# The last product of the attention units beside the chunks: 32-bit operands on half the rows, in place of three terms of split halves

## The chip, the cores and the metric

The kernel runs on one core of a Trainium2 chip. The metric is the device time of one execution in microseconds (us), from the host's side of the launch; lower is better. In the profile PE is the matrix engine (TensorE), PEld its weight loads, DVE is VectorE, ACT is ScalarE, POOL is GpSimd, SP is SyncE, whose queue issues most DMAs.

## The reference, cut to what matters

```python
def sm_attn(qq, kk, vv):
    s = scale * np.matmul(qq, kk.transpose(0, 1, 3, 2))
    s = s - np.max(s, axis=-1, keepdims=True)
    a = np.exp(s)
    a = a / (np.sum(a, axis=-1, keepdims=True) + 1e-09)
    return np.matmul(a, vv)
p_packed = sm_attn(p, k, v)                  # 32 packed rows per head
out = sm_attn(q, p_packed, p_packed)         # batch 8, heads 8, seq 576, head_dim 64
...
k = np.maximum(xk @ w_k, 0.0)                # MoE-like mixer on the attention's output
v = k * k @ w_v
r = 1.0 / (1.0 + np.exp(-(xr @ w_r)))
x = r * v
...
u = x + (x.transpose(0, 2, 1) @ U @ V).transpose(0, 2, 1)
out = u + np.maximum(u @ w_ch1, 0.0) @ w_ch2
```

The change concerns only the last product of the attention, `a @ p_packed`, and only in half of the attention units. All results are float32.

## The kernel before, in words

**Units.** A unit is a pair of batches times a pair of heads (two batches, two heads, 576 positions); there are 16. The first 8, the lead, run ahead of everything else, overlapped by `LAG`. They are called plain (`NPLAIN = 8`, L515). The other 8, units 8 to 15, run beside the chunks: at chunk 5 and at chunk 8 (L1392 to L1396) four units each are put into the program, and their instructions are laid between the matrix products of the chunks.

**Chunks.** The attention's output goes to DRAM (`x_d`) and comes back in 12 chunks of 384 positions. Each chunk has products into the accumulators `psr` (`r_block`, 128x512), `psk` (`k_block`, 128x384), `psv` (`v_block`, 128x512) and `psu` (`xu_block`, 128x512). After the chunks comes the second mixer (`psc`), which fills more than half of the time.

**Operand types.** The chunks' products take operands split in halves: a value is rounded to the type `F32R` (high half), the rest is a second `F32R` (low half), and `PASS` (L517) lists the three terms that are summed, high x high, high x low, low x high. One such term is one matmul instruction in the profile. A product with plain `F32` operands is one instruction in the program and two (each with its own weight load) in the profile.

**The end of a unit.** `pp` holds the packed rows of both batches and both heads, block-diagonal for the heads, batch 0 on partitions 0 to 63, batch 1 on 64 to 127. `th` holds the attention's shares, transposed, in the same partitions. In a plain unit (L841 to L846) each batch has one `F32` product that contracts over its own 64 partitions, so it uses 64 of the array's 128 rows, and the two batches use different rows. In a unit beside the chunks (L847 to L853) the product contracts over all 128 partitions with a weight matrix `wide` (`ppz`) in which the other batch's 64 rows are zero, so that it has the shape of a chunk's product, in three terms:

```python
for n, (lh, rh) in enumerate(((0, th), (0, tl), (1, th))):
    plan.mm(pss[b2][:, 0:w], ppz[:, lh, b2, :], rh[:, c0:c1], start=(n == 0), stop=(n == 2))
```

The 576 positions go in two pieces, 320 and then 256 (`halves`, L777), because a PSUM bank holds 512 columns; so a unit has 4 outputs (2 pieces x 2 batches) and 12 terms. Each output is copied from its bank to `xo` by ACT or DVE (L854), and `xo` is stored to `x_d` by one DMA (L856). What the three terms need beside the products: the halves of `pp` (L757 to L760), the halves of `th` (L828 to L832), and the zeros of `wide`, written once (L1024).

**What sets the order.** Nothing is issued as it is written. Every operation is recorded in a `Plan`, and `emit` (L341) replays the record as a list scheduler: it has a cost for each operation, takes on each engine the ready operation with the lowest class and place, and gives out PSUM banks as they come free. The attention units beside the chunks have two of the eight banks (`ps_a`). All matrix products are issued at L197 (transposes at L209), all ACT copies at L288, DVE copies at L291, DVE additions and subtractions at L254, DMAs at L319. The resulting order of each engine is fixed in the program; engines wait for each other by semaphores. The planner's cost of a matmul (L195 to L205) depends on the operands' type and on the number of rows and columns of the array that it uses, so the order of the whole program follows from these numbers.

Of the kernel before, what the change touches and what calls it, by code (L numbers as in the profile page):

```python
# [9 lines left out]
F32 = mybir.dt.float32  # L10
F32R = mybir.dt.float32r
I32 = mybir.dt.int32
U32 = mybir.dt.uint32
AF = mybir.ActivationFunctionType
# [463 lines left out]
def packed_attention_moe_mixer_kernel(  # L478
# [18 lines left out]
    B, H, S, D = q.shape  # L497
    NP = p.shape[2]
    P = 128
# [20 lines left out]
    plan = Plan(nc)  # L520
    add, sub, mul = ALU.add, ALU.subtract, ALU.mult

    def open_pool(es, name, bufs, side):
        return es.enter_context(tc.tile_pool(name=name, bufs=bufs, side=side, reuse_waits="tile"))
# [32 lines left out]
    def ps_att():  # L557
        return plan.bank(att_banks[0], "psat", att_banks[0] is ps_a)
# [17 lines left out]
    class Bufs:  # L576
        def __init__(self, es, name, side, nbig, first=False):
            self.big_p = Pool(obj=open_pool(es, name + "big", nbig, side), bufs=nbig)
            one = open_pool(es, name + "one", 1, side)
            self.one = Pool(obj=one, bufs=1)  # L580
            self.a1 = plan.fixed(one.tile([P, 640], F32, name="a1"))
            self.pbd = plan.fixed(one.tile([P, 2, D], F32, name="pbd"))
            self.st = plan.fixed(one.tile([P, 16], F32, name="st"), (0, 1))
            self.wide = None if first else plan.fixed(one.tile([P, 2, 2, P], F32R, name="wide"), (0, 1))
            self.first = first
            self.pools = [self.big_p, self.one]
            for f in (self.a1, self.pbd, self.st) + (() if first else (self.wide,)):
                f.alloc = plan.add((), lambda: None)
                self.one.tiles.append(f)
            self.kin, self.qin, self.vin, self.after = {}, {}, {}, ()  # L590
            plan.zero(self.a1[:, 512:640])
            plan.ts(self.st.at(1)[:, 7:8], self.a1[:, 512:513], 1e-9, None, add)
            self.kept = None

        def keep(self, plain):
            if self.kept is None or self.kept[0] != plain:
                pT = plan.tile(self.one, [P, 2, 64], F32, "pT")
                self.kept = (plain, pT, self.wide)
            return self.kept[1:]

        def tile_in(self, tag):
            return plan.tile(self.big_p, [P, 1152], F32, "big", parts=(0, 1, 2, 3), name=tag)
# [44 lines left out]
    def attention_steps(A, u, u_next):  # L647
# [5 lines left out]
        plain = u < NPLAIN  # L653
        kh = A.big(F32, "kh")
        qt, at = A.big(F32, "qt"), A.big(F32, "at", (0, 1))
        pT, ppz = A.keep(plain)

        def claim():
            A.kin[u_next], A.qin[u_next], A.vin[u_next] = [A.tile_in(n) for n in ("kin", "qin", "vin")]
# [27 lines left out]
        for b2 in range(2):  # L687
            for h in range(2):
                o = slice(b2 * 64 + h * 32, b2 * 64 + (h + 1) * 32)
                for r in range(2):  # L690
# [3 lines left out]
                            start=True, stop=True, skip_group_check=True)  # L694
# [15 lines left out]
        for b2 in range(2):  # L710
            r = slice(b2 * 64, (b2 + 1) * 64)
# [5 lines left out]
        for c in range(3):  # L717
# [5 lines left out]
            n = 3 if c < 2 or not plain else 2  # L723
            w = 8 if plain else NI
# [21 lines left out]
        for t in range(5):  # L746
            for g in range(4):
# [4 lines left out]
                        start=(t == 0), stop=(t == 4), skip_group_check=True)  # L752
        pp = plan.tile(A.one, [P, P], F32, "pp")
        plan.stt(pp.rearrange("p (h d) -> p h d", h=2), ps[:, 0:D].unsqueeze(1).to_broadcast([P, 2, D]),
                 s0[:, 9:10], hmask, mul, mul)
        if not plain:
            for b2 in range(2):  # L757
                r = slice(b2 * 64, (b2 + 1) * 64)
                plan.copy(ppz.at(b2)[r, 0, b2, :], pp[r])
                plan.tt(ppz.at(b2)[r, 1, b2, :], pp[r], ppz.at(b2)[r, 0, b2, :], sub)  # L760
        if early:
            A.load_v(u_next, A.after)
        yield
# [14 lines left out]
        if plain:  # L778
            yield
            psa = ps_att()  # L780
            for ip in range(4):
                for b2 in range(2):
                    plan.mm(psa[:, ip * P + b2 * 64:ip * P + (b2 + 1) * 64],
                            qt[:, b2 * 512 + ip * P:b2 * 512 + (ip + 1) * P],
                            ppt[:, b2 * 64:(b2 + 1) * 64], start=True, stop=True)
            yield
            psb = ps_att()
            plan.mm(psb[:, 0:P], qt[:, 1024:1152], ppt, start=True, stop=True)
            if A.first:
                a2 = A.big(F32, "a2", (0, 1))[:, 0:20 * NP].rearrange("p (g k) -> p g k", k=NP)  # L790
            else:
                a2 = plan.tile(A.one, [P, 20, NP], F32, "a2", parts=(0, 1))
            s2 = plan.tile(A.one, [P, 4, 20], F32, "s2", parts=(0, 1))
            for g, src, g0, g1 in ((0, psa, 0, 16), (1, psb[:, 0:P], 16, 20)):
                sv = src.rearrange("p (g k) -> p g k", k=NP)
                plan.reduce(s2.at(g)[:, 0, g0:g1], sv, ALU.max)
                plan.tt(a2.on(g)[:, g0:g1, :], sv,
                        s2.at(g)[:, 0, g0:g1].unsqueeze(2).to_broadcast([P, g1 - g0, NP]), sub)
            shares(a2, s2, 20)

            a2f = a2.rearrange("p g k -> p (g k)")
            th, tl = A.big(F32, "th"), None
            yield
            ps = ps_att()
            for ip in range(4):
                plan.transpose(ps[:, ip * P:(ip + 1) * P], a2f[:, ip * P:(ip + 1) * P], ident)
            plan.copy(th[:, 0:512], ps)
            yield
            ps = ps_att()
            plan.transpose(ps[:, 0:P], a2f[:, 512:640], ident)  # L810
            for b2 in range(2):
                r = slice(b2 * 64, (b2 + 1) * 64)
                plan.copy(th[r, 512:576], ps[r, r])
        else:
            n = S // NP
            a2 = plan.tile(A.one, [P, 20, NP], F32, "a2", parts=(0, 1))[:, 0:n, :]
            s2 = plan.tile(A.one, [P, 4, 20], F32, "s2", parts=(0, 1))
            for g, (c0, c1) in enumerate(halves):
                yield
                ps = ps_att()  # L820
                for b2 in range(2):
                    plan.mm(ps[b2 * 64:(b2 + 1) * 64, 0:c1 - c0], ppt[:, b2 * 64:(b2 + 1) * 64],
                            qt[:, b2 * S + c0:b2 * S + c1], start=True, stop=True, skip_group_check=True)
                plan.turn(a2.on(g)[:, c0 // NP:c1 // NP, :].rearrange("p g k -> p (g k)"), ps[:, 0:c1 - c0])
            plan.reduce(s2[:, 0, 0:n], a2, ALU.max)
            plan.tt(a2, a2, s2[:, 0, 0:n].unsqueeze(2).to_broadcast([P, n, NP]), sub)
            shares(a2, s2, n)
            tw = A.big(F32R, "th", (0, 1))  # L828
            th, tl = tw.at(0)[:, 0:S], tw.at(1)[:, S:2 * S]
            plan.turn(qt[:, 0:S], a2.rearrange("p g k -> p (g k)"))  # L830
            plan.act(th, qt[:, 0:S], AF.Copy)
            plan.tt(tl, qt[:, 0:S], th, sub)  # L832
            yield
        xo = A.big(F32, "xo", (0, 1)).rearrange("p (i b c) -> p i b c", i=NI, b=2)
        if u_next is not None and A.first:
            claim()
# [2 lines left out]
            A.load_v(u_next)  # L839
        for c0, c1 in halves:  # L840
            w = c1 - c0  # L841
            if plain:
                yield
                pss = [ps_att() for _ in range(2)]
                for b2 in range(2):
                    r = slice(b2 * 64, (b2 + 1) * 64)  # L846
                    plan.mm(pss[b2][:, 0:w], pp[r, :], th[r, c0:c1], start=True, stop=True)  # L847
            for b2 in range(2):
                if not plain:
                    yield  # L850
                    pss = {b2: ps_att()}
                    for n, (lh, rh) in enumerate(((0, th), (0, tl), (1, th))):
                        plan.mm(pss[b2][:, 0:w], ppz[:, lh, b2, :], rh[:, c0:c1], start=(n == 0), stop=(n == 2))  # L853
                plan.copy(xo.on(b2)[:, c0 // 64:c1 // 64, b2, :],  # L854
                          pss[b2][:, 0:w].rearrange("p (i c) -> p i c", c=64))
        x_last[0] = plan.dma(x_d[bp].at(j)[j * P:(j + 1) * P, :], xo.rearrange("p i b c -> p (i b c)"))  # L856
# [3 lines left out]
    def attention(A, u, u_next):  # L860
        for _ in attention_steps(A, u, u_next):
            pass
# [71 lines left out]
    A0 = Bufs(es_att, "A", "right", 8)  # L934
# [84 lines left out]
    for b2 in range(2):  # L1019
        r = slice(b2 * 64, (b2 + 1) * 64)  # L1020
        z = A0.a1[r, 513 - b2:577 - b2:2]
        plan.copy(ust[r].rearrange("p i (a c) -> p (i a) c", c=32),
                  z.unsqueeze(1).to_broadcast([64, NI * 4, 32]), ("dve",))
        plan.copy(A0.wide[r, :, 1 - b2, :].rearrange("p l (a c) -> p l a c", c=32),  # L1024
                  z.unsqueeze(1).unsqueeze(1).to_broadcast([64, 2, 4, 32]), ("dve",))
    usv = ust.rearrange("p i (a b r) -> p i a b r", a=2, b=2)
    uv = U.rearrange("(p i) r -> p (i r)", i=NI)
    for i0, i1 in ((0, NI),):
# [268 lines left out]
    bank_abc, first, acc = {}, set(), {}  # L1297
# [92 lines left out]
    for n in range(2, len(chunks)):  # L1390
        b, c = chunks[n]
# [63 lines left out]
    for q in range(NQ):  # L1455
# [11 lines left out]
        for f in range(NF):  # L1467
# [4 lines left out]
            a = product(q, f, 0, "a", True)  # L1472
# [5 lines left out]
            c = product(q, f, 2, "c", True)  # L1478
# [67 lines left out]
```

## Time and profile before

| | |
|---|---|
| median of 3 runs (lowest, highest) | 1498.82 us (1495.47 to 1500.59) |
| the profiled execution's own time | 1496.43 us |
| its span, first to last instruction | 1494.6 us |
| PE busy, PEld busy | 1462.0 us (98%), 1284.5 us (86%) |
| DVE, ACT, POOL busy | 926.5 us (62%), 685.7 us (46%), 269.1 us (18%) |
| share of PE in the chain that ended last | 92% |
| lead, chunks with attention, chunks alone, second mixer | about 0 to 137, 137 to 520, 520 to 700, 700 to 1495 us |

How to read it: a busy PE means that some matmul was in flight; a matmul's record is longer than its place in the stream, since it overlaps the next one. What a matmul costs the stream is read from the starts: the start of the next one less its own.

### The profile page before, as it was taken

The numbers are of one execution on the slowest core, as the hardware profiler recorded it, in microseconds if no ns is written. First come the engines' busy times: TensorE is split into PE (matmuls) and PEld (weight loads), VectorE is DVE, ScalarE is ACT, GpSimd is POOL, SyncE is SP. The second block draws the span as 40 slices with busy tenths as digits, with TensorE's granted clock in tenths as the row PEclk, the third lists the DMA queues.
The fourth block names the chain that finished last, engine by engine and source line by source line (L and its number), as shares of the span: only waits on it lengthen the run. The fifth ranks groups of instructions, "written<-read, shape, count | busy, mean of one in ns | idle before, by whom it ended". The sixth has DMA issues, their size and how long they took to land.

```text
span 1494.6 us, 25540 instructions
## 1 busy us (share of the span) xinstructions
PE 1462.0 (98%) x9336; PEld 1284.5 (86%) x9336; DVE 926.5 (62%) x2104; ACT 685.7 (46%) x1561; POOL 269.1 (18%) x522
## 2 busy tenths in 40 slices
PE   6899999999999999999999999999999999999998
PEld 5667888888888888888899999999999999999997
DVE  6777967888888888786544454544445454443533
ACT  5677666676666666775332322223232232322221
POOL 0000000000000000001333333333333233333331
PEclk8899999999999999999999999999999999999999
DMA  8963344654654448576969686686768667676763
GB/s 234 251 197 106 107 133 125 196 166 141 199 177 144 140 141 268 177 246 187 293 169 240 168 232 158 184 226 174 227 156 234 160 180 222 165 216 156 204 173 102
DMA packets 202188, 275.65 MB, mean 184 GB/s; under 512 B 68944, under 2 KB 95888, under 8 KB 202064
## 3 DMA queue, kind: packets, MB, share of 16 engines
q0 software_dynamic: 72576, 132.15, 33.5%
q1 hardware_dynamic: 129488, 141.87, 30.8%
q8 instruction: 75, 1.23, 0.3%
q14 instruction: 49, 0.40, 0.1%
HBM read 221.45 MB, written 52.50 MB: 183 GB/s over the span
## 4 chain that ended last, share of the span: by engine, by line
PE 92%; DMA 3%; DVE 2%; ACT 1%; SPq 1%; issue 1%; DVEq 0%; ACTq 0%
PE psc L197 50%; PE psk L197 13%; PE psv L197 13%; PE psr L197 7%; PE psat L197 4%; PE psat L209 3%; PE psh L197 1%; PE pst L209 1%; PE psu L197 1%; SPq L319 1%; DMA x_d<-xo 1%; DMA kin<-in_k_dram 1%; DMA s<-w_d 1%; DMA qin<-in_q_dram 1%; DMA prs<-x_d 0%
## 5 line engine op out<-in xcount | busy, mean ns | idle before, releaser
L197 PE MATMUL psc<-w,hid 128*128 128x512 f32 x1728 | 419.8, 391 | 0.7 <-ACT xu L288 0.7
L197 PEld LDWEIGHTS psc<-ob,wb 128*128 128x128 f32 x3024 | 388.3, 191 | 14.5
L197 PE MATMUL psc<-ob,wb 128*128 128x256 f32 x3024 | 398.8, 283 | 0.0
L319 POOL DMA_DIRECT2D wb<-ws_d x504 | 266.2, 528 | 580.2 <-PE psc L197 463.2
L197 PEld LDWEIGHTS psc<-w,hid 128*128 128x128 f32 x1728 | 315.3, 189 | 60.2 <-ACT xu L288 1.0
L254 DVE TENSOR_TENSOR tmp<-tmp,psc 128x256 f32<-128x256 f32 x288 | 120.3, 418 | 152.8 <-PE psc L197 150.6
L197 PE MATMUL psk<-xk,wk 128*128 128x384 f32 x1056 | 208.5, 340 | 1.2 <-ACT sq L233 0.8
L197 PE MATMUL psv<-wv,kk 128*128 128x512 f32 x783 | 202.0, 395 | 0.0
L233 ACT ACTIVATE hid<-tmp 128x256 fp32r<-128x256 f32 x216 | 85.7, 416 | 238.9 <-DVE tmp L254 238.9
L197 PEld LDWEIGHTS psk<-xk,wk 128*128 128x128 f32 x1056 | 184.6, 188 | 10.6 <-issue 1.5
L197 PEld LDWEIGHTS psv<-wv,kk 128*128 128x128 f32 x783 | 144.3, 188 | 28.3 <-issue 0.8
L273 DVE SCALAR_TENSOR_TENSOR hid<-psc,hid 128x256 fp32r<-128x256 f32 x72 | 30.5, 424 | 187.1 <-ACT hid L233 187.1
L197 PE MATMUL psr<-wr,xr 128*128 128x512 f32 x414 | 111.1, 401 | 0.1
L233 ACT ACTIVATE hid<-psc 128x256 fp32r<-128x256 f32 x72 | 27.4, 381 | 180.3 <-PE psc L197 180.3
L273 DVE SCALAR_TENSOR_TENSOR hid<-tmp,hid 128x256 fp32r<-128x256 f32 x216 | 87.2, 422 | 22.7 <-ACT hid L233 13.9
L311 POOL MEMSET x<- 128x8 f32 x4 | 0.4, 112 | 530.0 <-DVE m L270 529.7
L197 PEld LDWEIGHTS psr<-wr,xr 128*128 128x128 f32 x414 | 75.2, 188 | 18.3 <-issue 3.2
L233 ACT ACTIVATE sq<-psk 128x384 f32<-128x384 f32 x96 | 46.5, 489 | 69.1 <-PE psk L197 66.6
L288 ACT ACTIVATE tmp<-psc 128x256 f32<-128x256 f32 x144 | 54.3, 377 | 51.7 <-PE psc L197 51.7
L254 DVE TENSOR_TENSOR kk<-sq,kk 128x384 fp32r<-128x384 f32 x87 | 47.9, 553 | 33.7 <-ACT kk L288 33.4
L270 DVE SCALAR_TENSOR_TENSOR m<-x,mu_t,m 128x384 f32<-128x384 f32 x88 | 51.7, 611 | 1.1 <-ACT m L233 1.1
L233 ACT ACTIVATE m<-x,om_t 128x384 f32<-128x384 f32 x88 | 50.8, 607 | 2.7 <-DVE xr L254 1.8
(174 smaller groups left out, 1657.2 us busy)
## 6 DMA issues: line engine op xcount, KB each, us to landing
wb<-ws_d POOLq DMA_DIRECT2D x504, 256.0 KB, 3.5
st<-in_moe_w_ch_dram SPq DMA_DIRECT2D x32, 512.0 KB, 5.2
ws_d<-wb SPq DMA_DIRECT2D x56, 256.0 KB, 2.9
qin<-in_q_dram SPq DMA_DIRECT2D x32, 288.0 KB, 5.4
x_d<-xo SPq DMA_DIRECT2D x16, 576.0 KB, 3.5
x_d<-x SPq DMA_DIRECT2D x36, 256.0 KB, 2.1
u<-x_d SPq DMA_DIRECT2D x36, 256.0 KB, 5.3
out_dram<-u SPq DMA_DIRECT2D x36, 256.0 KB, 2.3
```

The lines of the kernel that those rows point to most:

```text
L197: self.nc.tensor.matmul(o, l, r, start=start, stop=stop, **k)
L209: self.nc.tensor.transpose(out.get(), in_.get(), ident.get())
L233: self.nc.scalar.activation(o, in_.get(), func, **k)
L254: return self.elem(engs, lambda e, o, x, y: e.tensor_tensor(out=o, in0=x, in1=y, op=op), out, [a, b], self.TT, cls)
L270: ("dve",), lambda e, o, x, y, z: e.scalar_tensor_tensor(out=o, in0=x, scalar=z, in1=y, op0=op0, op1=op1), out, [a, b, s], {"dve": (1.042, ...
L273: ("dve",), lambda e, o, x, y: e.scalar_tensor_tensor(out=o, in0=x, scalar=s, in1=y, op0=op0, op1=op1), out, [a, b], self.TT, cls)
L288: self.nc.scalar.activation(o, i, AF.Copy)
L311: (self.nc.gpsimd if eng == "pool" else self.nc.vector).memset(o, 0.0)
L319: (self.nc.sync if eng == "sp" else self.nc.gpsimd).dma_start(out=o, in_=i)
```

## The change

The units beside the chunks end like the plain ones. `wide`, its zeros, its halves and the halves of `th` go; the transposed shares are written to `th` directly as `F32`; each of the 4 outputs of a unit is one `F32` product over 64 rows, and the two batches of a piece are requested together, with two banks.

```diff
-            self.wide = None if first else plan.fixed(one.tile([P, 2, 2, P], F32R, name="wide"), (0, 1))
...
-        if not plain:
-            for b2 in range(2):
-                r = slice(b2 * 64, (b2 + 1) * 64)
-                plan.copy(ppz.at(b2)[r, 0, b2, :], pp[r])
-                plan.tt(ppz.at(b2)[r, 1, b2, :], pp[r], ppz.at(b2)[r, 0, b2, :], sub)
...
-            tw = A.big(F32R, "th", (0, 1))
-            th, tl = tw.at(0)[:, 0:S], tw.at(1)[:, S:2 * S]
-            plan.turn(qt[:, 0:S], a2.rearrange("p g k -> p (g k)"))
-            plan.act(th, qt[:, 0:S], AF.Copy)
-            plan.tt(tl, qt[:, 0:S], th, sub)
-            yield
+            th = A.big(F32, "th")
+            plan.turn(th[:, 0:S], a2.rearrange("p g k -> p (g k)"))
...
-            if plain:
-                yield
-                pss = [ps_att() for _ in range(2)]
-                for b2 in range(2):
-                    r = slice(b2 * 64, (b2 + 1) * 64)
-                    plan.mm(pss[b2][:, 0:w], pp[r, :], th[r, c0:c1], start=True, stop=True)
+            yield
+            pss = [ps_att() for _ in range(2)]
             for b2 in range(2):
-                if not plain:
-                    yield
-                    pss = {b2: ps_att()}
-                    for n, (lh, rh) in enumerate(((0, th), (0, tl), (1, th))):
-                        plan.mm(pss[b2][:, 0:w], ppz[:, lh, b2, :], rh[:, c0:c1], start=(n == 0), stop=(n == 2))
+                r = slice(b2 * 64, (b2 + 1) * 64)
+                plan.mm(pss[b2][:, 0:w], pp[r, :], th[r, c0:c1], start=True, stop=True)
+            for b2 in range(2):
                 plan.copy(xo.on(b2)[:, c0 // 64:c1 // 64, b2, :],
                           pss[b2][:, 0:w].rearrange("p (i c) -> p i c", c=64))
...
-        plan.copy(A0.wide[r, :, 1 - b2, :].rearrange("p l (a c) -> p l a c", c=32),
-                  z.unsqueeze(1).unsqueeze(1).to_broadcast([64, 2, 4, 32]), ("dve",))
```

Since the planner sees other costs, the order changes in more places than the diff shows. On PE, at the end of the first unit beside the chunks, the order before is this (`th` with `wide` are the three-term products of the unit, `psv` and `psr` the chunk's; x6 means six instructions in a row):

```order
L197 MATMUL psv<-wv_1865,kk 128x512 x3
L197 MATMUL psat<-th,wide 128x320 x2
L197 MATMUL psv<-wv_1865,kk 128x512
L197 MATMUL psr<-wr_184,xr 128x512 x2
L197 MATMUL psv<-wv_1865,kk 128x512 x2
L197 MATMUL psat<-th,wide 128x320 x4
L197 MATMUL psv<-wv_1865,kk 128x512 x3
L197 MATMUL psr<-wr_184,xr 128x512
L197 MATMUL psr<-wr_185,xr 128x512 x2
L197 MATMUL psat<-th,wide 128x256 x6
L197 MATMUL psr<-wr_185,xr 128x512
```

And this is PE at the end of the same unit with the change (`th` with `pp` are the 32-bit products; each is two instructions in a profile):

```order
L197 MATMUL psv<-wv_1873,kk 128x512 x7
L197 MATMUL psat<-th,pp 128x320 x2
L197 MATMUL psv<-wv_1873,kk 128x512 x2
L197 MATMUL psr<-wr_181,xr 128x512 x2
L197 MATMUL psat<-th,pp 128x256
L197 MATMUL psr<-wr_181,xr 128x512
L197 MATMUL psat<-th,pp 128x256
L197 MATMUL psr<-wr_182,xr 128x512 x3
```

The three groups of like-shaped terms became one pair for the piece of 320 and, for the piece of 256, two single products with a chunk's matmul between them. Five of the eight units have this form. In the other three (here the third) the piece of 256 is a pair too:

```order
L197 MATMUL psk<-xk,wk_0_185 128x384 x2
L197 MATMUL psat<-th,pp 128x320 x2
L197 MATMUL psk<-xk,wk_0_185 128x384
L197 MATMUL psk<-xk,wk_0_186 128x384 x3
L197 MATMUL psk<-xk,wk_0_187 128x384 x2
L197 MATMUL psat<-th,pp 128x256 x2
L197 MATMUL psk<-xk,wk_0_187 128x384
```

So all eight pieces of 320 stand as pairs, three pieces of 256 as pairs and five as two singles: 21 groups in the chunks' stream, each with chunk products on either side. In the lead the orders of PE, DVE and ACT differ from about a third of the lead on, with the same operations less the two zero copies of `wide`; the orders of SP's queue in the lead and of POOL's are the same.

## Rows read from the trace of the kernel before

**Rows 1.** Busy time by stretch: length, PE, PEld, DVE, ACT, POOL, clock, DMA share, GB/s.
```profile
60.00:137.00 77.00, 70.07 (x650) 50.25 (x649) 60.92 (x150) 57.56 (x155) 0.00 (x0) 0.99 0.59 173
137.00:520.00 383.00, 380.29 (x2442) 326.93 (x2443) 315.21 (x696) 256.20 (x538) 0.22 (x2) 1.00 0.50 154
```
**Rows 2.** Chain that ended last: start us, length us, what, matmuls in the piece.
```profile
205.73 5.44 PE psr L197 x24
...
357.00 2.10 PE psk L197 x12
```
**Rows 3.** Timeline of PE, 269.5 to 272 us: start, length, form, count, idle before.
```profile
269.33 0.63 PE L197 MATMUL psu<-xs,ust 128*128 128x512 f32 x2
270.47 0.50 PE L197 MATMUL psu<-xs,ust 128*128 128x512 f32 x1 [0.52 <-DVE xs L291]
271.41 0.50 PE L197 MATMUL psu<-xs,ust 128*128 128x512 f32 x1 [0.44 <-DVE xs L254]
271.74 0.51 PE L197 MATMUL psk<-xk,wk 128*128 128x384 f32 x2
```
**Rows 4.** Timeline of PE at the end of the first unit beside the chunks.
```profile
252.42 0.84 PE L197 MATMUL psv<-wv,kk 128*128 128x512 f32 x3
253.10 0.45 PE L197 MATMUL psat<-th,wide 128*128 128x320 f32 x2
253.39 0.39 PE L197 MATMUL psv<-wv,kk 128*128 128x512 f32 x1
...
254.55 0.75 PE L197 MATMUL psat<-th,wide 128*128 128x320 f32 x4
255.14 0.86 PE L197 MATMUL psv<-wv,kk 128*128 128x512 f32 x3
...
256.53 0.87 PE L197 MATMUL psat<-th,wide 128*128 128x256 f32 x6
257.24 0.88 PE L197 MATMUL psr<-wr,xr 128*128 128x512 f32 x3
```
**Rows 5.** Instructions on tile `wide`: count, duration ns min/median/max, first and last start.
```profile
L197 PE MATMUL psat<-th,wide x96: 277/294/313, 253.1 to 507.0; 128*128 128x320 f32 x48, 128*128 128x256 f32 x48
L254 DVE TENSOR_TENSOR wide<-pp,wide x16: 276/286/290, 238.7 to 489.5; 64x128 fp32r<-64x128 f32 x16
```
**Rows 6.** Instructions on tile `th`, same columns: its halves.
```profile
L233 ACT ACTIVATE th<-qt x8: 668/676/687, 250.2 to 502.8; 128x576 fp32r<-128x576 f32 x8
L254 DVE TENSOR_TENSOR th<-qt,th x8: 751/756/760, 252.1 to 503.5; 128x576 fp32r<-128x576 f32 x8
```
**Rows 7.** Timeline of PE where the last plain unit ends between chunk products.
```profile
134.73 1.03 PE L197 MATMUL psk<-xk,wk 128*128 128x384 f32 x5
135.69 1.24 PE L197 MATMUL psat<-th,pp 64*128 64x320 f32 x8
136.87 0.45 PE L197 MATMUL psk<-xk,wk 128*128 128x384 f32 x1
137.15 0.34 PE L197 MATMUL psk<-xr,wk 128*128 128x384 f32 x1
```
**Rows 8.** Timeline of PE, another plain unit: the pair of 320.
```profile
108.64 0.81 PE L197 MATMUL psat<-th,pp 64*128 64x320 f32 x4
109.38 0.50 PE L197 MATMUL psr<-wr,xr 128*128 128x512 f32 x1
109.72 0.38 PE L197 MATMUL psat<-ppt,qt 128*128 128x128 f32 x2
```
**Rows 9.** Timeline of PE, another plain unit: the pair of 256.
```profile
119.42 0.70 PE L197 MATMUL psat<-th,pp 64*128 64x256 f32 x4
120.05 0.50 PE L197 MATMUL psr<-wr,xr 128*128 128x512 f32 x1
```
**Rows 10.** Timeline of PE, another plain unit: 256 as two singles.
```profile
83.52 1.40 PE L197 MATMUL psat<-th,pp 64*128 64x256 f32 x4 [0.28 <-ACT xo L288]
84.86 0.96 PE L197 MATMUL psr<-wr,xr 128*128 128x512 f32 x3
```

More of the change, by code (lines that the diff above doesn't have):

```diff
@@ L583, in __init__ @@
             self.st = plan.fixed(one.tile([P, 16], F32, name="st"), (0, 1))
-            self.wide = None if first else plan.fixed(one.tile([P, 2, 2, P], F32R, name="wide"), (0, 1))
             self.first = first
             self.pools = [self.big_p, self.one]
-            for f in (self.a1, self.pbd, self.st) + (() if first else (self.wide,)):
+            for f in (self.a1, self.pbd, self.st):
                 f.alloc = plan.add((), lambda: None)
@@ L593, in __init__, with keep @@
             self.kept = None
[L595 to L599, printed above, removed]
+        def keep(self):
+            if self.kept is None:
+                self.kept = plan.tile(self.one, [P, 2, 64], F32, "pT")
+            return self.kept
         def tile_in(self, tag):
@@ L655, in attention_steps @@
         qt, at = A.big(F32, "qt"), A.big(F32, "at", (0, 1))
-        pT, ppz = A.keep(plain)
+        pT = A.keep()
         def claim():
@@ L801, in attention_steps @@
             a2f = a2.rearrange("p g k -> p (g k)")
-            th, tl = A.big(F32, "th"), None
+            th = A.big(F32, "th")
             yield
@@ L827, in attention_steps @@
             shares(a2, s2, n)
-            tw = A.big(F32R, "th", (0, 1))
-            th, tl = tw.at(0)[:, 0:S], tw.at(1)[:, S:2 * S]
-            plan.turn(qt[:, 0:S], a2.rearrange("p g k -> p (g k)"))
-            plan.act(th, qt[:, 0:S], AF.Copy)
-            plan.tt(tl, qt[:, 0:S], th, sub)
-            yield
+            th = A.big(F32, "th")
+            plan.turn(th[:, 0:S], a2.rearrange("p g k -> p (g k)"))
         xo = A.big(F32, "xo", (0, 1)).rearrange("p (i b c) -> p i b c", i=NI, b=2)
```

## The prediction

> **What bounds the kernel now.** I read first the busy time by stretch, then the chain that ended last, then the timeline of PE around the products that change. In the stretch from 137 to 520 us, where all eight changed units end, PE is busy 380.29 of 383 us at the full clock, 2.4 GHz, while DVE has 315 and ACT 256 us of work [rows 1]. The chain goes through PE piece by piece: twelve `psk` products in 2.10 us (0.175 each), 24 `psr` products in 5.44 us (0.227 each) [rows 2]. So PE's stream is the clock of this stage, and of the stages behind it: a microsecond put into the stream or taken from it moves the end by a microsecond. Idle time is small but dearer than it looks. Where three `psu` products wait for DVE, 0.96 us of idle are shown, but from the first start to the next product's start 2.41 us pass for what should take 3 x 0.23 = 0.69, so 1.72 us are lost [rows 3]: a stopped pipeline is also refilled. The 2.7 us of idle in the stretch [rows 1] thus stand for an estimated 2.7 x 1.72 / 0.96 = 4.8 us.
>
> **What goes from PE.** There are 96 three-term products [rows 5], 12 per unit. By starts, in the first unit: 253.10 to 253.39, 254.55 to 255.14 and 256.53 to 257.24, that is 0.29 + 0.59 + 0.71 = 1.59 us [rows 4]. Their borders are free: the three `psv` ahead of them take 0.68, or 0.227 each, the usual pace [rows 4]. Eight units: 12.7 us removed.
>
> **What comes to PE.** The price of a 32-bit product on 64 rows is shown by the plain units. Three things are to be seen.
>
> First, two products of different batches run side by side. Two products of 320 are four instructions and take 0.74 us from the first start to the next product [rows 8]; two of 256 take 0.63 [rows 9]. Two singles of 256, one after the other, take 1.34, or 0.67 each, of which a little is a wait; I take 0.65 [rows 10]. So a single costs as much as a pair: pairing gives one product free, and a planner that parts a pair pays it twice.
>
> Second, each group has borders. Ahead of the eight instructions of the last plain unit, five `psk` take 0.96 us where 5 x 0.175 = 0.875 are usual: 0.09 to get in. Behind them the first `psk` takes 0.28 in place of 0.175, 0.11 to get out [rows 7]; behind the pair of 320 a `psr` takes 0.34 in place of 0.227, again 0.11 [rows 8]. Together 0.20 us per group.
>
> Third, how many groups there are is in the changed order, shown above: 8 pairs of 320, 3 pairs of 256, 10 singles of 256.
>
> | groups | each | us |
> |---|---|---|
> | 8 pairs of 320 | 0.74 + 0.20 | 7.5 |
> | 3 pairs of 256 | 0.63 + 0.20 | 2.5 |
> | 10 singles of 256 | 0.65 + 0.20 | 8.5 |
> | added | | 18.5 |
> | removed | | 12.7 |
> | **net on PE** | | **+5.8** |
>
> Had the planner kept all four products of a unit in one run, they would take 1.17 + 0.20 = 1.37 us [rows 7], and the sum would be 8 x (1.37 - 1.59) = -1.8 us. The products alone are no dearer; that they come in 21 groups is.
>
> On the borders a page bears. The Trainium skill, TensorEngine Tiling (Array Packing), section Tiling Modes, says that a change of the tiling mode drains the engine, which speaks against this change, since each group goes from 128 rows to 64 and back. The rows agree, at 0.20 us a group; were that rule not in force here, 21 x 0.20 = 4.2 us would fall away and the net would be +1.6.
>
> **What goes from DVE and ACT.** Per unit DVE loses one subtraction on `th` (0.756 us [rows 6]) and two on `wide` (0.286 each [rows 5]), ACT one copy to `th` (0.676 [rows 6]), and two copies of `pp`'s high half fall away on one or the other, at most about the 0.286 of the subtraction on the same shape. That is some 1.3 us of DVE and 1 us of ACT per unit, 10 and 8 us in a stretch in which both have over 65 us to spare [rows 1]. On the path it is worth nothing of itself: PE does chunk products meanwhile. The two zero copies of `wide` in the lead go too. What it can give is part of the 4.8 us lost to waits, so the bounds are 0 and -4.8; I take 0, since the order of DVE and ACT is drawn anew as well and new waits are as likely.
>
> **What waits are added.** The two batches of a piece now ask for both of the unit's banks at once, so the products of 256 wait until the 320s have been copied to `xo`. That wait is in rows 10: 0.28 us, for ACT's copy. Queued behind it on PE would be the chunk products. In the changed order two to six of these stand between, 0.7 us or more, so I take 0; the other bound is 8 x 0.28 = 2.2 us.
>
> **The lead.** From about a third of it on, PE, DVE and ACT run in another order. PE is idle 6.9 of the 77 us from 60 to 137 [rows 1], waiting for DVE and ACT in small pieces. No row prices the new order; the operations are the same, so I take 0 and bound it by half of that idle time, 3.5 us, both ways. DMAs are the same in number and size; `x_d` is stored once per unit as before, and the chunk that reads it comes three chunks later.
>
> **The sum.** +5.8 us on a profiled execution of 1496.4 us. The median shown is 2.4 us above that execution; I put the sum on the median, 1498.8 + 5.8 = **1504.6 us**, 0.39% slower. About 0.3%, 4.5 us, is what a measurement of this kernel can tell from no change.
>
> **Rivals.**
> - **Relief of DVE and ACT** (not slower). Place: the `psu` products that wait for `xs` from DVE, and the other waits from 137 to 520. For it: DVE is busy 82% of that stretch and loses 10 us; and PE, being longer in each unit than before, gives the other engines more time. Against it: the waits come from a fixed order, and their number is small. If all went: +5.8 - 4.8 = +1.0, 1499.8 us. From a relief of 1.3 us on, the result is within 0.3%. Chance 0.21.
> - **Only the streamed columns count.** If the engine lays the borders of the groups over the neighbouring products, and parted pairs still overlap, a unit costs what the unbroken run costs, 1.17 us [rows 7]: 8 x (1.17 - 1.59) = -3.4, 1495.4 us. Against it: three of three borders in rows 7 and 8 cost 0.09 or 0.11. Chance 0.05. The Trainium skill, FP8 and Floating Point Precision, section TensorE Precision Notes, gives true FP32 four passes through the array; an estimate from it, with both batches side by side, is 4 x 576 columns at 2.4 GHz, 0.96 us a unit, and 8 x (0.96 - 1.59) = -5.0, 1493.8 us. No row of this case is as short.
> - **The lead decides.** The new order of the lead closes or opens half of its idle time: +5.8 less or plus 3.5, so 1501.1 or 1508.1 us. For it: the lead is the one place where engines wait for each other. Against: the same operations, the same DMA order. Chance 0.16, half each way.
> - That the change does not do what it says is excluded by the order: 32 products of `th` with `pp` stand there, none with `wide`.
>
> **How the numbers follow.** The forecast has 0.58, the rivals 0.21, 0.05 and 0.16. Slower by over 0.3%: 0.52 of the forecast's 0.58 (5.8 is not far above 4.5, and medians of runs move by a microsecond or so) and 0.08 of the lead: 0.60. Within 0.3%: 0.06 of the forecast, 0.21 of the relief, 0.08 of the lead, 0.02 of the columns: 0.37. Faster: the other 0.03 of the columns. The range takes in the relief nearly whole and the added wait or a bad lead above: 1498.5 to 1509.0. The forecast's own range is 1502 to 1507.
>
> **What would show it.** In the profile after: 64 instructions of `psat<-th,pp` on 64 rows beyond 137 us; pairs at 0.74 and 0.63 us by starts, singles at about 0.63; the chunk product behind each group 0.11 us longer; the attention stretch longer by 5 to 6 us while the stretches behind it keep their lengths; DVE about 11 us and ACT about 8 us less busy. I would be wrong if pairs ran together where chunk products stand between them, if groups had free borders, or if idle PE time between 137 and 520 us fell to nothing or rose by several microseconds.

## The result and the profile after

The change is slower. In six runs of each kernel its median is 1506.84 us (1505.38 to 1512.0) against 1497.93 us (1494.21 to 1500.59), a ratio of 1.0061 with a 95% interval of 1.0045 to 1.0076. Measured once more (12 runs, beside 17 of the kernel before) it gave 1503.58 against 1499.26 us, ratio 1.0028 [1.0010, 1.0046]. Both medians lie in the range given, on either side of the forecast of 1504.6 us; whether the loss is above or below 0.3%, the two measurements leave open. One execution further down, of the run with pairs kept, took 3310 us; its median and ratio are those of the other eleven.

The page of the profiled execution, whose own time is 1506.4 us, its head and busy times:

```profile
span 1504.3 us, 25440 instructions
PE 1472.4 (98%) x9304; PEld 1279.6 (85%) x9304; DVE 920.5 (61%) x2077; ACT 675.1 (45%) x1536; POOL 270.5 (18%) x522
```

Its busy time by stretch, columns as in [rows 1]:

```profile
60.00:137.00 77.00, 70.97 (x619) 48.78 (x619) 58.48 (x144) 54.18 (x147) 0.00 (x0) 0.91 0.56 170
137.00:520.00 383.00, 381.03 (x2398) 315.84 (x2397) 306.17 (x663) 244.63 (x512) 0.23 (x2) 1.00 0.50 151
```

From 137 to 520 us DVE has 9.0 and ACT 11.6 us less to do than in [rows 1] (about 11 and 8 were forecast), and PE is as full as it was. The groups stand as the changed order had them. Instructions on tile `th` (the 64 of the lead are among the 128), and the timeline of PE at the end of the first unit, which answers to [rows 4]:

```profile
L197 PE MATMUL psat<-th,pp x128: 376/480/810, 35.6 to 495.8; 64*128 64x320 f32 x64, 64*128 64x256 f32 x64
```

```profile
255.37 0.81 PE L197 MATMUL psat<-th,pp 64*128 64x320 f32 x4
256.11 0.72 PE L197 MATMUL psv<-wv,kk 128*128 128x512 f32 x2
256.67 0.63 PE L197 MATMUL psr<-wr,xr 128*128 128x512 f32 x2
257.23 0.70 PE L197 MATMUL psat<-th,pp 64*128 64x256 f32 x2
257.86 0.50 PE L197 MATMUL psr<-wr,xr 128*128 128x512 f32 x1
258.29 0.70 PE L197 MATMUL psat<-th,pp 64*128 64x256 f32 x2
258.91 0.96 PE L197 MATMUL psr<-wr,xr 128*128 128x512 f32 x3
259.71 0.60 PE L209 MATMUL psat<-ident,kin 128*128 128x128 f32 x4
```

The pair of 320 takes 0.74 us by its starts and the two `psv` behind it 0.56, 0.11 above their usual 0.45, as in [rows 8]. Around the two singles: `psr` x2 0.56, single 0.63, `psr` 0.43, single 0.62, `psr` x3 0.80. Less six usual `psr` (1.36) that is 1.68 us, 0.84 for each single with its borders, where [rows 10] and the borders had given 0.85.

Where the 9.7 us between the two profiled spans (1504.3 and 1494.6) came from, by the starts of the first `psk` product, of the first `psr` of chunk 8, and of the first and the 201st `psc` product:

| stretch | before | after | difference |
|---|---|---|---|
| lead, to the first `psk` | 133.14 | 136.42 | +3.3 |
| attention stretch, to the first `psr` of chunk 8 | 391.40 | 394.86 | +3.5 |
| chunks alone, to the first `psc` | | | 0.0 |
| seam: the first 200 `psc` of the second mixer | 36.47 | 39.12 | +2.65 |
| the rest | | | +0.2 |

The seam is the time from the first `psc` to the start of the 201st, in each kernel. Chunks are counted from 0; the eight units are put into the program at chunks 2 and 5 (L1392 to L1396), not at 5 and 8 as was said above. Only the second line is the stage whose products the prediction priced. The experiments were chosen to find which of the three are the change's own.

### The profile page after: what moved, and what is told of

Read it like the earlier page. It is cut to its first block, busy times and chain, and to the rows that moved or that the text cites. A ratio compares the mean times of both kernels' runs of the same rounds, so it can differ in the third digit from the quotient of the medians.

```text
span 1504.3 us, 25440 instructions
## 1 busy us (share of the span) xinstructions
PE 1472.4 (98%) x9304; PEld 1279.6 (85%) x9304; DVE 920.5 (61%) x2077; ACT 675.1 (45%) x1536; POOL 270.5 (18%) x522
## 4 chain that ended last, share of the span: by engine, by line
PE 93%; DMA 3%; DVE 1%; SPq 1%; ACT 1%; issue 1%; DVEq 0%
PE psc L197 50%; PE psk L197 13%; PE psv L197 13%; PE psr L197 7%; PE psat L197 4%; PE psat L209 3%; SPq L319 1%; DMA kin<-in_k_dram 1%; PE psh L197 1%; PE pst L209 1%; PE psu L197 1%; DMA s<-w_d 1%; DMA vin<-in_v_dram 0%; DMA qin<-in_q_dram 0%; DVE a L273 0%
## 5 line engine op out<-in xcount | busy, mean ns | idle before, releaser
L197 PEld LDWEIGHTS psk<-xk,wk 128*128 128x128 f32 x1056 | 184.9, 188 | 12.7 <-issue 2.6
```

The lines of the kernel that those rows point to most:

```text
L197: self.nc.tensor.matmul(o, l, r, start=start, stop=stop, **k)
```

## The experiments

**Is it the lead's order?** The change drops two DVE copies in the lead, and the planner then orders the lead anew. The first two runs part these: the change with the lead's old order, and the kernel before with the new one. Neither leaves out any of the computation.

The first keeps `wide` and its two zero copies, which nothing reads:

```diff
+            self.wide = None if first else plan.fixed(one.tile([P, 2, 2, P], F32R, name="wide"), (0, 1))
...
+        plan.copy(A0.wide[r, :, 1 - b2, :].rearrange("p l (a c) -> p l a c", c=32),
+                  z.unsqueeze(1).unsqueeze(1).to_broadcast([64, 2, 4, 32]), ("dve",))
```

> The changed kernel, but the tile wide and its two zero copies on DVE stay in the lead (nothing reads them). With them the planner draws the lead in the order of the kernel before, while the units beside the chunks end with the 32-bit products. Theory: of the 8.9 us by which the change is slower, about 3 come from the newly drawn lead (the first psk starts at 136.4 us after the change, 133.1 before) and the rest from the products and what follows; so the first psk is back at 133 us and the time is 1503 to 1505 us, 5 to 7 above the kernel before. Rival: the order of the lead is worth nothing, the two leads differ by chance from execution to execution, and the time stays at about 1507 us.

Measured: 1504.29 us, ratio to before 1.0031 [1.0015, 1.0047]; lead 136.65, attention stretch 394.48, seam 39.38 us. The lead did not come back to 133 us. The stretch is longer by 3.1 us with the old order of the lead too, so most of its 3.5 us do not come from that order.

The second moves the zero copies of the kernel before to POOL:

```diff
-                  z.unsqueeze(1).unsqueeze(1).to_broadcast([64, 2, 4, 32]), ("dve",))
+                  z.unsqueeze(1).unsqueeze(1).to_broadcast([64, 2, 4, 32]), ("pool",))
```

> The kernel before, with its three-term ends, but the two zero copies of wide are made by POOL, so that DVE's and PE's order in the lead is that of the changed kernel. Theory: the new lead alone costs about 3 us, so the first psk starts at about 136 us and the time is 1500 to 1502 us against 1498. Rival: the order of the lead is worth nothing, and the time is that of the kernel before within 1 us.

Measured: 1502.31 us, ratio 1.0011 [0.9993, 1.0030]; lead 140.48, stretch 392.51, seam 37.13 us. The stretch grew by 1.1 us without one changed product. The waits of PE from 137 to 535 us (engine, tile, line, releaser, us in all, times, longest) tell why, first the kernel before, then the change; the first line of the change stands in this run word for word the same. The third list is the run with the zeros kept, its two lines on `psu`:

```profile
PE psu L197 <- DVE xs L291: 1.0, 2, 0.5
PE psk L197 <- ACT sq L233: 0.8, 2, 0.4
PE psk L197 <- DVE wk L273: 0.4, 1, 0.4
PE psu L197 <- DVE xs L254: 0.4, 1, 0.4
```

```profile
PE psk L197 <- DVE wk L273: 1.6, 2, 1.0
PE psk L197 <- ACT sq L233: 0.4, 1, 0.4
```

```profile
PE psu L197 <- DVE xs L291: 0.5, 1, 0.5
PE psu L197 <- DVE xs L254: 0.2, 1, 0.2
```

The new lead makes `psk` products of the first two chunks, 35 us behind the first `psk`, wait 1.2 us longer for the cast of `wk`. Up to the first `psr` of chunk 2 PE loses by it about 1.4 us against the kernel before (1.36 to 1.41) in every run with the new lead, and at most 0.03 us in the others. In the change the `psu` waits of [rows 3] are gone. The third list says that the lighter units alone do not do that: with the same units and the lead's old order, 0.7 us of them are left.

**Is it that pairs are parted?** Here the first product of a pair also waits in the planner until both banks are granted, so that no chunk product comes between the two:

```diff
-                plan.mm(pss[b2][:, 0:w], pp[r, :], th[r, c0:c1], start=True, stop=True)
+                o = plan.mm(pss[b2][:, 0:w], pp[r, :], th[r, c0:c1], start=True, stop=True)
+                if not plain:
+                    plan.gates.append((o, pss[1].alloc))
...
+        for op, bank in self.gates:
+            op.preds[bank] = 1
```

> The changed kernel, but beside the chunks the first product of a piece waits until both banks are granted, so the planner cannot part the two batches: 8 pairs of 320 and 8 pairs of 256, 16 groups in place of 21. The lead's order is that of the changed kernel. Theory: a single costs as much as a pair (0.83 us with its borders), so five groups less take 5 x 0.83 = 4.1 us from PE's stream, and the time is about 1502.7 us. Rival: what parts the pairs is hidden or is only moved, because the second bank is waited for: no change from 1506.8 us, with new idle time of PE ahead of the pairs.

Measured: attention stretch 390.98 us, 3.9 less than with the change and 0.4 less than before. Timeline of PE at the first unit's end:

```profile
257.92 1.09 PE L197 MATMUL psr<-wr,xr 128*128 128x512 f32 x4
258.94 0.70 PE L197 MATMUL psat<-th,pp 64*128 64x256 f32 x4
259.57 1.20 PE L197 MATMUL psr<-wr,xr 128*128 128x512 f32 x4
```

All 16 pieces are now pairs, five groups fewer than 21. Five singles of 0.82 saved are 4.1 us; the stretch shows 3.9. So parting is most of what made the units' new end dearer than the old one, 4.1 us of 5.55 (below). It is not all: the 16 pairs still take 8 x 0.94 + 8 x 0.83 = 14.2 us by starts where the terms took 12.65, and the stretch is no longer than before only because PE waits less in it. The whole kernel gained less: 1502.36 us, ratio 1.0015 [0.9996, 1.0035], with a lead of 137.66 and a seam of 39.29 us.

**What is late at the seam?** Timeline of PE in the change where the second mixer's first pass turns to its second batch, then ACT there, and the same place of PE before:

```profile
722.47 0.39 PE L197 MATMUL psc<-w,hid 128*128 128x512 f32 x1
724.65 2.04 PE L197 MATMUL psc<-w,hid 128*128 128x512 f32 x5 [1.79 <-ACT xu L288]
```

```profile
723.49 0.63 ACT L288 ACTIVATE w<-s 128x512 fp32r<-128x512 f32 x1 [3.43 <-DMA s<-w_d]
724.02 0.58 ACT L288 ACTIVATE xu<-psu 128x512 f32<-128x512 f32 x1
```

```profile
715.71 0.39 PE L197 MATMUL psc<-w,hid 128*128 128x512 f32 x1
716.79 1.43 PE L197 MATMUL psc<-w,hid 128*128 128x512 f32 x5 [0.68 <-ACT xu L288]
```

PE waits for the copy `xu`, the copy stands on ACT behind a cast of weights, and the cast waits for their DMA. After the longer wait the granted clock fell. Busy times of the change by stretch, from 725 us:

```profile
725.00:729.00 4.00, 4.00 (x17) 3.57 (x16) 2.32 (x6) 2.06 (x5) 0.62 (x2) 0.57 1.14 387
729.00:733.00 4.00, 4.00 (x26) 3.60 (x25) 2.40 (x6) 1.50 (x4) 0.97 (x2) 1.00 1.12 401
```

The 0.57 is a mean: (1 - 0.57) x 4 / 0.5 = 3.4 of these 4 us were at 1.2 GHz. There 17 products ran in 4 us where 26 ran in the next 4. The wait's extra 1.1 us and 0.43 x 4 = 1.7 us of clock make 2.8, the seam's 2.65. The run meant to take the copy out from behind the cast:

```diff
-            plan.copy(xu, ups[0])
+            plan.copy(xu, ups[0], ("act", "dve") if b + 1 < NBP else ("dve",))
```

> The changed kernel, but the last copy of the xu accumulator is made by DVE and not by ACT, where it stood behind a weight copy that waited for its DMA. Theory: the wait of the first psc products for that copy (1.8 us of idle time, and half the clock from 725 to 729 us behind it) goes, so the seam gives back 2 to 2.7 us: about 1504.3 us. Rival: DVE stands behind the same DMA, so the wait is only moved: 1506.8 us.

Measured: 1507.38 us, ratio 1.0043 [1.0026, 1.0060]; seam 39.20 us. The wait is only moved, as the rival had it: PE now stops a little later for another ACT copy behind the same cast. Waits of PE, 700 to 740 us:

```profile
PE psc L197 <- ACT tmp L288: 1.8, 1, 1.8
```

So the DMA is what is late, not the copy that stood behind it. **Does it come with the kernel?** Both kernels ran again, unaltered.

> The changed kernel unaltered, for a ratio with more runs and a second trace, on the same chip as the next three. If the parts measured so far add up (0.31% for the ends with the lead of before, 0.11% for the lead) the ratio is about 1.0045, inside the interval of the first measurement; if the interval's middle holds it is 1.006. In the trace the steps beside the chunks and the step at the first psc products (+2.6 us) recur to 0.1 us, and only the lead differs.

> The kernel before unaltered, one look for a second trace. Theory: the lead differs by chance by a few us (the first psk started at 133.1 us in the first trace, at 136.7 in a kernel with the same lead), so 133 to 137 us here; beside the chunks and at the first psc products the trace repeats to 0.1 us, the wait for the xu copy 0.7 us. Rival: the first psk is at 133 us again, and the wait at the first psc products varies from run to run.

The change gave the 1503.58 us quoted above (its profiled execution 1507.59), with lead 140.04, stretch 394.87 and seam 36.80 us; the kernel before gave 1500.26 us (one run), with 136.74, 391.44 and 36.67 us. The stretch repeats within 0.04 us in both. The seam's 2.65 us do not repeat in the change, and the lead moved by 3.6 us in both.

**What sets the seam?** In the change, beside the loads of that burst, one more transfer runs: a fetch of 16 KB, which the queue's name in the trace calls instructions. DMA queues in the window 711 to 719 us of the change (transfers, MB, share of the 16 engines):

```profile
q8 instruction: 1, 0.02, 0.8%
```

In both traces of the kernel before it comes 4.4 and 4.5 us ahead of the first `psc`; in the change 7.6 us behind it, among the loads. If its place follows from the number of instructions, some more of them ahead of the seam would move it out of the burst. So 32 tiny products, which nothing reads, were put into chunk 9:

```diff
+        if n == 9:
+            pad = plan.bank(ps_a, "pad")
+            for _ in range(32):
+                plan.mm(pad[0:32, 0:32], half(wr[0], 0)[:, 0:32], half(wr[0], 0)[:, 0:32], start=True, stop=True)
```

> The changed kernel with 32 tiny products on PE (32x32, into a spare bank, read by nobody) in chunk 9, so that PE has the number of instructions of the kernel before when it comes to the second mixer. Theory: the 2.6 us at the first psc products come from where PE's code is fetched (a 16 KB transfer on queue 8 starts at 707.3 us in the changed kernel, in the middle of a burst of loads on which the ACT queue waits; at 695.3 in the kernel before); with the pad the fetch is ahead of the burst again, and the wait for the xu copy is 0.7 to 1.3 us and not 1.8, without a drop of the clock: the step is 0 to 0.7 us. Rival: the wait has another cause, and the step stays at 2.6 to 2.9 us.

Measured (one run): 1505.94 us; the fetch comes 4.6 us ahead of the first `psc`, as before the change, and the seam is 36.34 us. Timeline of PE there:

```profile
726.00 1.45 PE L197 MATMUL psc<-w,hid 128*128 128x512 f32 x5 [0.53 <-ACT xu L288]
```

The wait is 0.53 us. (In the change the fetch starts at 714.1 us; the 707.3 in the text above is wrong.) All traces with this order of PE at the seam (with `xu` on DVE it differs a little), by where the fetch starts against the first `psc`, with the wait of PE there:

| run | matmuls | fetch, us | wait, us | seam, us |
|---|---|---|---|---|
| kernel before | 9336 | -4.4 | 0.68 | 36.47 |
| kernel before, again | 9336 | -4.5 | 0.87 | 36.67 |
| zero copies on POOL | 9336 | -3.0 | 1.32 | 37.13 |
| pad | 9336 | -4.6 | 0.53 | 36.34 |
| change, again | 9304 | +8.7 | 1.00 | 36.80 |
| change | 9304 | +7.6 | 1.79 | 39.12 |
| zeros kept | 9304 | +7.8 | 2.07 | 39.38 |
| pairs kept | 9304 | +7.6 | 1.93 | 39.29 |
| `xu` on DVE | 9304 | +8.0 | 1.79 | 39.20 |
| 32-bit products on all rows (below) | 9304 | +7.4 | 1.89 | 39.20 |

The place of the fetch follows the number of PE's instructions, and the pad moved it. The seam is dear in the five traces in which the granted clock fell behind the wait, after 1.79 to 2.07 us of idle; it did not fall after 0.53 to 1.32. All five have the fetch among the loads, but the second run of the change has it there too and a cheap seam, and the waits of the two groups overlap. So the fetch is a likely cause of the longer wait and not a shown one, and the pad, which ran once, does not settle it. How a transfer of 16 KB could delay the loads by over 1 us, no run shows.

**Is it the 32-bit type or the 64 rows?** The 32-bit products were put on all 128 rows, with the other batch's rows of the weights zero as before the change:

```diff
+            self.wide = None if first else plan.fixed(one.tile([P, 2, P], F32, name="wide"), (0, 1))
...
+                plan.copy(A.wide.at(b2)[r, b2, :], pp[r])
...
+                    plan.mm(pss[b2][:, 0:w], A.wide.at(b2)[:, b2, :], th[:, c0:c1], start=True, stop=True)
```

> The 32-bit products of the change on all 128 rows: pp of each batch stands in an F32 tile whose other 64 rows are zero (two copies per unit, zeros once in the lead), so nothing runs side by side, and the array is used as for the chunk products. Theory: the 0.09 us to get in belong to the change of 128 rows to 64, not to the 32-bit type (F32 transposes on 128 rows show 0.00 to 0.01), so getting in costs 0.01 and getting out about 0.09 us per group; a product of 320 takes twice 320 x 2 columns, 0.53 us, one of 256 takes 0.43, a pair twice that, and a unit 1.92 + 0.1 x 2.5 groups = 2.2 us, 17 to 18 us for eight, no more than the change's 18.2 although every product uses the engine alone. Rival: the border belongs to the 32-bit type, and a group pays 0.20 us as with 64 rows.

Measured (one run): 1501.92 us, attention stretch 393.04, seam 39.20 us. Timeline of PE at two units' ends:

```profile
251.45 1.24 PE L197 MATMUL psat<-th,wide 128*128 128x320 f32 x4
252.29 0.86 PE L197 MATMUL psv<-wv,kk 128*128 128x512 f32 x2
252.99 0.59 PE L197 MATMUL psat<-th,wide 128*128 128x256 f32 x2
253.23 0.81 PE L197 MATMUL psr<-wr,xr 128*128 128x512 f32 x2
253.88 0.59 PE L197 MATMUL psat<-th,wide 128*128 128x256 f32 x2
...
326.12 1.02 PE L197 MATMUL psat<-th,wide 128*128 128x256 f32 x4
326.80 0.70 PE L197 MATMUL psk<-xk,wk 128*128 128x384 f32 x2
327.33 0.40 PE L197 MATMUL psu<-xs,ust 128*128 128x512 f32 x1
```

From group to chunk product and on to the next piece, less the usual pace of the chunk products: two of 320 cost 0.84 + 0.70 - 0.45 = 1.09 us, one of 256 costs 0.24 + 0.65 - 0.45 = 0.44, two cost 0.68 + 0.53 - 0.35 = 0.86. These follow the columns alone: two singles cost what a pair costs, and by these prices the eight units take 15.6 us, where 17 to 18 had been expected. On 64 rows the same work costs 0.94, 0.83 and 0.83. If the two products of a pair run fully side by side there, they need half of 1.09 or 0.86, and what is left is the same for all three kinds of group: 0.94 - 0.54, 0.83 - 0.43 and 0.83 - 0.44 are all about 0.40 us. The last is the single, which has nothing beside it and needs no such "if"; and the unbroken run of four, 1.37 with its borders [rows 7], leaves 1.37 - 0.54 - 0.43 = 0.40 as well. So a group on 64 rows pays some 0.40 us for going there and back, and the 32-bit type has no such price. The same products on all rows, one after the other, are cheaper than the change's 18.2 us (summed below), though nothing in them runs side by side.

**Can the old form be made shorter?** The low half of the shares need not have a product of its own. Per batch the high half goes on the batch's own 64 rows and the low half on the rows where `wide` had zeros, with the weights' high half beside both; the same three terms are then two products on 128 rows:

```diff
+                plan.copy(ppz.at(b2)[(1 - b2) * 64:(2 - b2) * 64, 0, b2, :], pp[r])
...
-                    for n, (lh, rh) in enumerate(((0, th), (0, tl), (1, th))):
-                        plan.mm(pss[b2][:, 0:w], ppz[:, lh, b2, :], rh[:, c0:c1], start=(n == 0), stop=(n == 2))
+                    for n in range(2):
+                        plan.mm(pss[b2][:, 0:w], ppz.at(b2)[:, n, b2, :], th[b2][:, c0:c1], start=(n == 0), stop=(n == 1))
```

> A version from what PE's stream showed: from the kernel before, but both halves of the shares of a batch are put one above the other on the 128 rows, so that a unit's output needs two terms of 128 rows and not three (the high half of pp on all rows, then the low half on 64 of them). 8 products per unit in place of 12, no borders, one more copy on ACT or DVE and one more on each for the halves. Theory: PE's stream loses a third of 12.7 us, 4.2 us, and the time is 1494 to 1496 us. Rival: DVE and ACT, 82% and 67% busy beside the chunks, cannot take 2.5 us more per unit, and PE waits: 1498 us or more.

Measured: 1493.11 us (1491.54 to 1497.66), ratio to before 0.9960 [0.9945, 0.9976], the one version that beats both kernels. Instructions on `wide`, which answer to [rows 5]:

```profile
L197 PE MATMUL psat<-th,wide x64: 276/294/386, 257.9 to 514.4; 128*128 128x320 f32 x32, 128*128 128x256 f32 x32
```

64 in place of 96, each as short as before: a third of 12.7 us, 4.2. The attention stretch is 386.74 us, 4.7 less than before; at the seam, whose order is another in this kernel, the first `psc` starts 2.1 us later and the next 200 take 3.0 less. The term saved is most of the gain of the stretch; of the seam's 1 us no run shows the cause.

## Why the prediction was right, and where it was not

**The products: right.** Summed over the trace of the change, the 21 groups with their borders take 18.2 us (forecast 18.5), against 12.65 removed (12.7): +5.55 for +5.8. The pairs of 320 measured 0.93 to 0.94, the pairs of 256 0.83, the singles 0.82 us. That parting a pair is what costs was said, and the run with pairs kept shows it: 3.9 us.

**The borders: half-sized.** The prediction put 0.20 us a group on the chunk products on either side and took the rest for work. The products on 128 rows show 0.40. Half lay inside the group's own 0.63 or 0.74. The sum was not hurt, since the price was the group's as a whole, but the text beside the rule was: without the borders the net would not be +1.6 but 18.2 - 21 x 0.40 - 12.65 = -2.9 us, an estimate from these rows, near the second rival's -3.4. The Trainium skill, TensorEngine Tiling (Array Packing), section Tiling Modes, names the drain at a change of tiling mode. These runs agree: the price, 0.40 us a group, appears with 64-row products among 128-row ones and not with 32-bit products on 128 rows.

**"What it can give is part of the 4.8 us lost to waits ... I take 0": this term was mis-sized.** It measured -2.0 us: the loss to waits, counted over the stretch by starts as in [rows 3], went from 4.75 to 2.8. Two parts make it. Relief is real, some -3.3 us at the `psu` products of [rows 3]; and a new wait of +1.4 us for the cast of `wk`, which the run with the zero copies on POOL ties to the lead's new order, not to the units. The rival of relief was thus right in its place and in about two thirds of its price; whether by its reason, less work on DVE and ACT, is open, since with the lead's old order the same units keep 0.7 us of these waits. The working of the 4.8 has a slip: from 269.33 to 271.74 us [rows 3] show four `psu` products (x2, x1, x1), not three, so 2.41 - 4 x 0.23 = 1.5 us are lost there, and the estimate would have been 4.2. Counted over the whole stretch the loss before is 4.75, so the bound stood. The stretch: 5.55 - 2.0 = +3.55 worked out, +3.5 measured, where 5 to 6 had been named.

**Added bank wait: right.** Taken at 0; no wait of a 64-row product for a copy to `xo` stands among the waits of PE from 137 to 535 us.

**The lead: still open.** It was taken at 0, bounded by 3.5. With the old order the first `psk` starts at 133.14, 136.74, 136.65 and 137.00 us, with the new one at 136.42, 140.04, 140.48, 137.66, 135.49 and 137.75 (the 32-bit products on all rows have a third order, 133.90). The means are 135.9 and 138.0, but the values overlap, and they move with the granted clock. Busy times from 20 to 140 us, the two traces of the kernel before, then the two of the change (the column behind POOL's is the clock):

```profile
20.00:140.00 120.00, 102.51 (x938) 76.28 (x937) 92.67 (x228) 83.49 (x230) 0.00 (x0) 0.91 0.71 199
```

```profile
20.00:140.00 120.00, 104.02 (x932) 74.12 (x932) 92.64 (x228) 80.93 (x223) 0.00 (x0) 0.89 0.67 193
```

```profile
20.00:140.00 120.00, 103.34 (x919) 74.73 (x917) 92.00 (x224) 80.30 (x224) 0.00 (x0) 0.89 0.67 193
```

```profile
20.00:140.00 120.00, 106.28 (x910) 75.16 (x911) 90.94 (x224) 78.71 (x218) 0.00 (x0) 0.84 0.67 194
```

One kernel's lead differs by 3.6 us between two executions. The second and the third row have the same clock, 0.89, one with the old and one with the new order, and there the leads are 136.74 and 136.42; with the zeros kept (old order) and with pairs kept (new order), both at 0.87, they are 136.65 and 137.66. At one clock the new order costs 1 us at most. Whether it lowers the clock (0.83 to 0.89 with it, 0.87 to 0.91 with the old one) is what stays open. The whole-kernel ratio of the run that has the new lead and the old products, 1.0011 [0.9993, 1.0030], includes no cost.

**"The stretches behind it keep their lengths": wrong at one place.** The chunks alone kept theirs, but the second mixer's start took up to 2.65 us more where PE waited longer for its loads and the clock fell. That does not explain why the two measurements differ, 1.0061 and 1.0028: of the change's two profiled executions the one with the cheap seam took longer, 1507.59 against 1506.40 us. What goes with the times is the granted clock of the whole execution, 0.987 in the middle of the first six runs of the change and 0.991 in the middle of the twelve later ones, and within the twelve the time goes with it, from 1498.65 us at 0.993 to 1510.0 at 0.985. What lowered the clock in the first six, no run shows. So the forecast's 1504.6 us fell between the two medians partly by luck, through terms that cancelled: waits gave 2.0 us back, and lead and seam, both put at nothing, took some.

## What to carry to other kernels

Each visit from full-row products to products on half of the array's rows costs a fixed price, so count the visits in the planned order, not the products. Here 21 visits cost 5.55 us more than the old terms and 16 visits, all pairs, still 1.5; only one visit a unit would have been cheaper, an estimate from the 1.37 us of [rows 7]. Where zeros fill the other half of the rows, put the second term there before changing the type or the tiling. And when a stream is made longer or shorter, look one stage behind too: a burst of loads may meet something there that moves with the code's length.

## What the runs showed of the hardware that was not expected

- A group of 64-row products among 128-row products pays about 0.40 us whatever its length (32-bit products on all 128 rows pay nothing of the kind), of which 0.20 us shows in the neighbours' starts and the rest in its own.
- Where a fetch of 16 KB of instructions starts follows the number of PE's instructions: 3.0 to 4.6 us ahead of the first `psc` with 9336 matmuls, 7.4 to 8.7 behind it with 9304, and 32 more in chunk 9, whose results nothing reads, moved it. In the burst of weight loads it goes with waits of PE of 1.00 to 2.07 us, ahead of it with 0.53 to 1.32.
- After 1.79 us of idle PE (1.79 to 2.07 in five traces) the granted clock was at the lower of its two levels, 1.2 GHz, for 3.4 us, so that a wait longer by 1.1 us made the stage longer by 2.65.
